# Decode kernel on one core: output weights loaded in wider rows with the attention output regrouped to match, half a head of them moved behind the last values, the last piece halved, the second K load in one piece, x loaded a second time

## The chip, the core and the metric

The kernel runs on one core of a Trainium2 chip. The metric is the device time of one execution in microseconds (us). A page called "the profile" is one execution taken by the hardware profiler; its span is about 2 us shorter than the time of the same execution. In this document PE is the matmul engine, DVE and ACT the two elementwise engines, SP the engine that issues nearly all loads.

## The reference, cut to what matters

One decode step: layer norm of one row x (448 wide), an attention over a cache of 65536 positions with 16 query heads in 8 K/V heads of width 256, an output projection, and a small gated feed-forward on the same row.

```python
xn = _layernorm(A_x)
q  = xn @ wq                                   # 448 -> 16 x 256
o  = softmax(q k^T / 16) v                     # k_cache, v_cache: 8 x 65536 x 256, bf16
y  = (silu(xn @ w_gate) * (xn @ w_up)) @ w_down * sigmoid(xn @ w_r)
out = x + o.reshape(1, 4096) @ wo + (xn + y)   # wo: 4096 x 448
```

K and V together are 537 MB of the 549 MB that are read. Every byte is used once.

## The kernel before

One ring of three 8 MB slots takes the loads: two slots for K, one for V (names in the code: `NT` = 28 value loads of the first seven heads, `U` = 4 loads of K for a head). SP issues all of them in order on one queue, each after a wait for the slot to come free. The first K loads come in two halves so that PE can start early:

```python
def k_item(u):
    need = [("FREE", u - 2)] if u >= 2 else ()
    if 2 <= u < UH:                                   # UH = 5: loads 0..4 are halved
        need = {0: [("FREEH", u - 2)], 1: need}
    slot_item("k", u, u % 2, [("slot%d" % (u % 2), CH), ("half%d" % (u % 2), CH)] if u < UH else None, need)
```

At the end the freed V slot takes the feed-forward weights and the output weights of seven heads, one load a head. The rows of one head are spread so that partition p holds rows p*2 and p*2+1 of each of the two query heads: two runs of 2 x 448 x 2 = 1792 bytes.

```python
def wo_src(h):
    return A_wo[h * rep * Dh:(h + 1) * rep * Dh, :].rearrange("(i p f) n -> p i f n", i=rep, f=NH)
...
slot_item("v", NT, 0, None, [("FREE", NU - 2)])
item("wg", ...gate and up weights...)
item("wd", ...two loads...)
item("wo", [(wo_view(wo_all[:, h * WON:(h + 1) * WON]), wo_src(h), "wo") for h in range(Hkv - 1)])
slot_item("v", NT + 1, ...); slot_item("v", NT + 2, ...)
slot_item("v", NT + 3, 2, ...six pieces of 64, 32, 16, 8, 4, 4 rows..., [("ATTN",), ("FFN2",)])
for i in range(rep):                                  # eighth head: two pieces, the very last loads
    item(("wo_end", i), [(wo_view(wo_end)[:, i, :, :], wo_src(Hkv - 1)[:, i, :, :], "we%d" % i)], ...)
```

Behind the last values come the last steps: normalise the attention output (tile oT_sb), multiply it with the eighth head's weights into ps_s ("the last matmuls"), copy the result, store it.

## Time and profile before

| | before |
|---|---|
| time, median (lowest to highest) | 1278.09 us of 3 runs (1277.79 to 1279.21); 1278.49 with the next three |
| span of the profile | 1276.0 us |
| DMA row, 40 slices | 9 in 39 of 40, then 8 |
| packets of 1792 bytes | 2048 of about 12,200 data packets |
| values' last landing / last weights' landing / result copy | 1272.23 / 1273.36 / 1273.98 us |

From the page: the DMA row of the 40 slices (tenths of the time that the 16 DMA engines were busy), the packet counts, and the chain of waits, followed back from the last instruction.

```profile
DMA  9999999999999999999999999999999999999998
...
DMA packets 13588, 549.20 MB, mean 430 GB/s; under 512 B 1414, under 2 KB 3464, under 8 KB 4104
...
DMA 76%; PE 19%; SPq 2%; ACT 1%; issue 1%; DVE 1%; ACTq 0%; DVEq 0%
```

The loads fill the span. The trace also records every packet (start, duration, size) and, for every load, the landing on each of the 16 engines. In the packet records the 16 engines hold a packet from about 1.8 us to 1272 us. One packet of 65536 bytes takes 2.422 us on the mean, and none of the 7424 in this trace took less than 2.418, so the 16 move 433 GB/s with such packets; over the whole span it was 430. There is next to nothing to win but packet cost, idle engines at the start, and the tail.

The timeline of SP as the feed-forward and output weights are issued (start, duration, engine, operation; merged rows):

```profile
1183.56 0.91 SPq L883 DMA_DIRECT2D ring<-in_B_w_down_dram  x2
1184.51 19.69 SPq L883 DMA_DIRECT2D ring<-in_A_wo_dram  x7
1204.24 0.99 SPq L883 DMA_DIRECT2D ring<-in_A_v_cache_dram  x1
```

It looks as if 19.69 us of issuing were a cost. But in the packet records at least 16 packets were under way at every moment of that time, mostly of loads issued earlier. So SP's standing there cost the loads nothing. The first two of the seven issues took 0.43 and 0.47 us, the third 7.16; that the queue had no room for more is my reading.

The timeline of PE, its weight loads (PEld) and DVE at the end (the square brackets tell the idle time before the row and what ended it; some rows left out):

```profile
1272.28 0.38 PE L412 MATMUL ps_m<-p_sb,ring 128*128 128x2 bf16 x8 [0.25 <-DMA ring<-in_A_v_cache_dram]
...
1272.80 0.16 DVE L654 TENSOR_TENSOR oT_sb<-ps_m,rs 128x4 bf16<-128x4 f32 x1 [0.48 <-PE ps_m L412]
...
1273.02 0.92 PE L412 MATMUL ps_s<-kt_all,oT_sb 128*1 128x224 bf16 x8 [0.25 <-DVE oT_sb L654]
1273.40 0.09 PEld L412 LDWEIGHTS ps_s<-kt_all,oT_sb 128*1 128x1 bf16 x4 [0.30 <-DMA kt_all<-in_A_wo_dram]
...
1273.98 0.38 DVE L835 CAST kt_all<-ps_s 33x224 bf16<-33x224 f32 x1 [1.02 <-PE ps_s L412]
```

The eight last matmuls start when the attention is ready (oT_sb); the second four of them start at 1273.40, when the last weights have landed (1273.36). Both arrive together, within about 0.1 us.

### The profile page before, as it was taken

The page shows a single profiled execution, that of the slowest core. Times are in us where ns is not written, and L with a number is a line of the kernel's source. Part 1 is how long each engine was busy: PE and PEld are TensorE (multiplying, and loading weights), DVE is VectorE, ACT ScalarE, POOL GpSimd, SP SyncE. Part 2 cuts the span into 40 slices and gives each one's busy share as a digit, 9 for nine tenths or more (in the row PEclk, how much of TensorE's full clock was granted, in tenths as well). Part 3 has the DMA queues.
Part 4 walks back from the last instruction along what each step waited for, and adds up shares of the span by engine and source line. Part 5 has one row for each costly group of instructions (what it writes and reads, how often), then busy time and mean ns, then how long its engine had stood idle before and what let it go on. Part 6 is the DMA issues. An engine that isn't in the chain of part 4 may idle for free.

```text
span 1276.0 us, 23620 instructions
## 1 busy us (share of the span) xinstructions
PE 976.1 (76%) x9791; PEld 638.2 (50%) x9791; DVE 570.2 (45%) x1079; ACT 436.6 (34%) x655; POOL 8.0 (1%) x38
## 2 busy tenths in 40 slices
PE   4998888778777679767778776787777688777674
PEld 3676655455544456444555454455454455454321
DVE  4665554355444455343454344454344554444310
ACT  1554533244333334323333342343333334332300
POOL 2000000000000000000000000000000000000000
PEclk9998999799888898887898888898888998888885
DMA  9999999999999999999999999999999999999998
GB/s 405 430 428 440 437 431 436 431 429 440 433 429 438 427 440 433 431 438 427 436 436 431 438 429 431 438 431 431 438 427 438 436 431 438 427 436 438 409 434 360
DMA packets 13588, 549.20 MB, mean 430 GB/s; under 512 B 1414, under 2 KB 3464, under 8 KB 4104
## 3 DMA queue, kind: packets, MB, share of 16 engines
q1 hardware_dynamic: 13570, 549.03, 99.7%
q8 instruction: 8, 0.13, 0.0%
q14 instruction: 4, 0.03, 0.0%
q10 hardware_dynamic: 6, 0.00, 0.0%
HBM read 549.03 MB, written 0.00 MB: 430 GB/s over the span
## 4 chain that ended last, share of the span: by engine, by line
DMA 76%; PE 19%; SPq 2%; ACT 1%; issue 1%; DVE 1%; ACTq 0%; DVEq 0%
DMA ring<-in_A_v_cache_dram 70%; PE ps_o L412 13%; DMA ring<-in_A_k_cache_dram 5%; PE ps_t L412 3%; SPq L883 2%; PE ps_m L412 2%; PE ps_q L412 2%; ACT kt_all L482 1%; DMA ring<-in_A_wo_dram 1%; DVE kt_all L480 0%; ACT S_sb L563 0%; PE ps_s L412 0%; DVE kt_all L699 0%; DVE m1p L533 0%; DVE kt_all L835 0%
## 5 line engine op out<-in xcount | busy, mean ns | idle before, releaser
L412 PE MATMUL ps_t<-ident_f,ring 128*128 128x128 f32 x4096 | 590.0, 286 | 71.9 <-DMA ring<-in_A_k_cache_dram 48.3
L480 DVE COPY kt_all<-ps_t 128x1024 bf16<-128x1024 bf16 x768 | 486.9, 684 | 285.8 <-PE ps_q L412 281.2
L412 PEld LDWEIGHTS ps_t<-ident_f,ring 128*128 128x128 f32 x4096 | 453.9, 144 | 227.6 <-issue 139.8
L482 ACT ACTIVATE kt_all<-ps_t 128x1024 bf16<-128x1024 bf16 x256 | 262.2, 1024 | 507.0 <-PE ps_q L412 506.9
L412 PE MATMUL ps_o<-ring,p_sb 128*4 128x512 bf16 x2044 | 186.9, 531 | 195.6 <-DMA ring<-in_A_v_cache_dram 191.3
L412 PEld LDWEIGHTS ps_o<-ring,p_sb 128*4 128x4 bf16 x2044 | 55.2, 105 | 289.5 <-issue 265.7
L412 PE MATMUL ps_q<-kt_all,q_cur 128*2 128x512 bf16 x2056 | 164.7, 397 | 0.6 <-DVE kt_all L480 0.6
L504 ACT ACTIVATE s<-ps_q 98x512 bf16<-98x512 f32 x257 | 151.8, 591 | 1.3 <-PE ps_q L412 1.3
L588 DVE RECIPROCAL rs<-ps_m 128x4 f32<-128x4 f32 x29 | 5.3, 183 | 271.8 <-PE ps_m L412 271.8
L573 ACT ACTIVATE p_sb<-S_sb 128x128 bf16<-128x128 bf16 x64 | 18.9, 307 | 266.2 <-PE ps_o L412 266.0
L412 PEld LDWEIGHTS ps_s<-sel_bf,s 128*128 128x128 bf16 x1032 | 64.2, 97 | 6.3 <-ACT s L504 1.9
L412 PE MATMUL ps_s<-sel_bf,s 128*128 128x8 bf16 x1032 | 63.4, 167 | 2.3 <-ACT s L504 1.3
L631 DVE CAST ob_sb<-ps_o 100x512 bf16<-100x512 f32 x29 | 20.1, 692 | 100.7 <-PE ps_o L412 100.7
L412 PEld LDWEIGHTS ps_q<-kt_all,q_cur 128*2 128x2 bf16 x2056 | 26.4, 79 | 45.5 <-issue 45.5
L412 PEld LDWEIGHTS ps_m<-rowsum,ones_f 128*128 128x128 f32 x116 | 20.1, 246 | 20.5 <-issue 20.5
L412 PE MATMUL ps_m<-rowsum,ones_f 128*128 128x2 f32 x116 | 22.5, 299 | 0.0
L533 DVE TENSOR_REDUCE m1p<-S_sb (+1 forms) x33 | 13.9, 422 | 4.4
L482 ACT ACT_TABLE_LOAD x7 | 9.0, 1283 | 19.1 <-PE ps_q L412 19.1
L531 DVE CAST S_sb<-ps_s 128x256 f32 (+1 forms) x33 | 13.6, 414 | 1.9 <-PE ps_s L412 1.9
L563 ACT ACTIVATE S_sb<-S_sb,negmax 128x512 bf16<-128x512 bf16 x16 | 13.2, 852 | 3.0 <-DVE negmax L557 3.0
L412 PE MATMUL ps_m<-diag,ones_f 2*128 2x2 f32 x58 | 11.0, 256 | 3.7 <-DVE diag L548 0.6
L412 PEld LDWEIGHTS ps_m<-diag,ones_f 2*128 2x128 f32 x58 | 8.5, 182 | 10.5 <-DVE diag L548 10.5
(94 smaller groups left out, 129.3 us busy)
## 6 DMA issues: line engine op xcount, KB each, us to landing
ring<-in_A_k_cache_dram SPq DMA_DIRECT2D x10, 4096.0 KB, 35.1
ring<-in_A_v_cache_dram SPq DMA_DIRECT2D x1, 4096.0 KB, 30.9
ring<-in_A_wq_dram SPq DMA_DIRECT2D x1, 3584.0 KB, 11.3
ring<-in_A_wo_dram SPq DMA_DIRECT2D x7, 448.0 KB, 17.1
ring<-in_A_v_cache_dram SPq DMA_DIRECT2D x1, 2048.0 KB, 35.5
ring<-in_B_w_gate_dram SPq DMA_DIRECT2D x1, 1568.0 KB, 14.9
ring<-in_B_w_up_dram SPq DMA_DIRECT2D x1, 1568.0 KB, 18.3
ring<-in_B_w_down_dram SPq DMA_DIRECT2D x2, 784.0 KB, 20.5
```

The costliest lines, as they stand in the source:

```text
L412: return pe.matmul(*a, **k)
L480: O(e, ("EV", s, m), lambda it: nc.vector.tensor_copy(out=kt[:, :], in_=tb[:, :]), f"ev{m}")
L482: O(e, ("EV", s, m), lambda it: nc.scalar.activation(out=kt[:, :], in_=tb[:, :], func=ACTF.Copy), f"ev{m}")
L504: O("act", ("EVQ", s), lambda it: nc.scalar.activation(out=s2[s % 2][0:QROWS, :], in_=ps_q[0:QROWS, :], func=ACTF.Copy), "evq")
L531: O("dve", ("SCOPY", u), lambda it: nc.vector.tensor_copy(out=S_sb[:, at(it, SBN), :], in_=ps_sn), "sc")
L533: O("dve", ("SMAX", u), lambda it: nc.vector.tensor_reduce(out=m1p[:, :, at(it, 1)], in_=S_sb[:, at(it, SBN), :].rearrange("p n i -> p i n ...
L563: O("act", ("EXP", h, i), lambda it, i=i: nc.scalar.activation(out=S_sb[:, :, i], in_=S_sb[:, :, i], func=ACTF.Exp, bias=negmax[:, i:i + 1 ...
L573: O("act", ("PC", t, c), lambda it: nc.scalar.activation(out=p_sb[:, c, :, :], in_=S_sb[:, n:n + CH, :], func=ACTF.Copy), "pc")
L588: O("dve", ("RS", t), lambda it: nc.vector.reciprocal(out=rs[:, :, :], in_=ps_m[0:P, C_TOT:C_TOT + NH * rep]))
L631: O("dve", ("OB", t), lambda it: nc.vector.tensor_copy(out=ob_sb[0:OROWS, :], in_=ps_o[0:OROWS, :]))
L883: eng.dma_start(fn[0], fn[1]).then_inc(sems[sem], 16)
```

## The change

Its intent: fewer and larger packets, the attention's last steps hidden behind loads, and two matmuls instead of four behind the very last load. Core of the diff, cuts marked:

```diff
+    HALVED = (0, 2, 3, 4)
...
-        if 2 <= u < UH:
+        if u >= 2 and u in HALVED:              # second K load whole; its half semaphore is preset
-        ... if u < UH else None, need)
+        ... if u in HALVED else None, need)
+    semtot = {"half1": 16}; items[("k", 1, 1)] = ("half1", 16)
...
+    def wo_rows(h0, h1):                        # partition p: four neighbouring rows, 3584 bytes
+        return A_wo[h0 * rep * Dh:h1 * rep * Dh, :].rearrange("(h p f) n -> p h f n", p=P, f=FO)
...
-    item("wd", ...two loads...)
-    item("wo", ...seven loads in runs of 1792 bytes...)
+    item("wd", [...one load..., (x_again, A_x[0], "wd")])
+    item("wo", [...six heads in one load..., ...first half of the seventh head...])
...
-    slot_item("v", NT + 3, 2, ..., [("ATTN",), ("FFN2",)])
+    slot_item("v", NT + 3, 2, ..., [("SUM",)])
+    item("wx", [...second half of the seventh head...], [("HT",)])
+    ENDS = [(0, 0, NH), (1, 0, 1), (1, 1, NH)]  # eighth head: three pieces instead of two
+    for k, (i, f0, f1) in enumerate(ENDS):
+        item(("wo_end", k), [...])
...
-        O("dve", "OTH", ...copy of oT_f...)
+        O("pe", "REGROUP", ...8 small matmuls with every second column of the identity...)
+        O("dve", "OTH", ...copy of the regrouped tile...)
...
+        O("dve", "XN_AGAIN", ...); O("dve", "YX", ...)   # x and its norm added here
-        base column: 4 matmuls at the start, 4 at the end, 3 vector steps (removed)
-        TOT: two matmuls for each value load's row sums
+        TOT: one
```

The base column held x and its norm for the final sum.

More of the change, by code (lines that the diff above doesn't have):

```diff
@@ L76, in bass_parallel_sum__gqa_block_cached__moe_arch_mod__decode_kernel @@
     WQN, WGN, WDN, WON = RP * HqDh // 2, RP * F, FH * D, rep * NH * D
+    FO = rep * NH
     WOA = (Hkv - 1) * WON
-    assert WOA + WGN + 2 * WDN <= SLOT
+    WEN = WOA + WGN + 2 * WDN
+    assert WEN + 2 * D <= SLOT
     DC = D // 4
@@ L95, in bass_parallel_sum__gqa_block_cached__moe_arch_mod__decode_kernel @@
     wd_area = slots[2][:, WOA + WGN:WOA + WGN + 2 * WDN]
+    x_again = slots[2][0:1, WEN:WEN + D]
+    xn_again = slots[2][0:1, WEN + D:WEN + 2 * D]
     wo_end = kt_all[:, 0:WON]
@@ L129, in bass_parallel_sum__gqa_block_cached__moe_arch_mod__decode_kernel @@
     oT_f = S_("oT_f", [P, NH, Hkv - 1, rep], FP32)
-    oT_h = S_("oT_h", [P, NH, Hkv - 1, rep], BF16)
-    base_c = S_("base_c", [P, 4], FP32)
+    oT_h = S_("oT_h", [P, FO, Hkv - 1], BF16)
     KB = 2 * FB
@@ L138, in bass_parallel_sum__gqa_block_cached__moe_arch_mod__decode_kernel @@
     res_bf = kt_all[:, 3 * KB + 2 * D:3 * KB + 2 * D + DQ]
-    assert WON <= 2 * KB and 3 * KB + 2 * D + DQ <= NKT * 8 * P
+    wo_x = kt_all[:, 2 * KB:2 * KB + WON // 2]
+    assert WON // 2 <= KB and WON <= 2 * KB and 3 * KB + 2 * D + DQ <= NKT * 8 * P
     hT_sb = S_("hT_sb", [P, FH, 2], BF16)
@@ L143, in bass_parallel_sum__gqa_block_cached__moe_arch_mod__decode_kernel @@
     x_f, xc_f, xn_f = T_(D, FP32), T_(D, FP32), T_(D, FP32)
-    xnb_f = xc_f
-    base_f = xn_f
     xn_bf = T_(D)
@@ L166, in bass_parallel_sum__gqa_block_cached__moe_arch_mod__decode_kernel @@
     C_HT = C_Q
-    C_BASE = C_Q
     assert C_Q + NH * Hq + 4 <= C_BIG and C_HT + FK <= C_BIG and C_BIG + P <= 512
@@ L177, in SEM @@
         return name
-    for n_ in ["pe", "act", "dve", "pool", "qk", "jt", "evq", "exp", "pc", "qc", "sc", "w0", "out", "wq", "wg", "wo", "wd", "we0", "we1", "half0", "half1"]:
+    for n_ in ["pe", "act", "dve", "pool", "qk", "jt", "evq", "exp", "pc", "qc", "sc", "w0", "out", "wq", "wg", "wo", "wd", "we0", "we1", "we2", "wx", "half0", "half1"]:
         SEM(n_)
@@ L234, in bass_parallel_sum__gqa_block_cached__moe_arch_mod__decode_kernel @@
     late = []
-    semtot = {}
+    semtot = {"half1": 16}
+    items[("k", 1, 1)] = ("half1", 16)
     fed = {}
@@ L262, in flat_src, with wo_src, wo_at @@
         return src.rearrange("a b -> (a b)").rearrange("(p n) -> p n", p=P)
-    def wo_src(h):
-        return A_wo[h * rep * Dh:(h + 1) * rep * Dh, :].rearrange("(i p f) n -> p i f n", i=rep, f=NH)
+    def wo_src():
+        return A_wo[(Hq - rep) * Dh:Hq * Dh, :].rearrange("(i p f) n -> p i f n", i=rep, f=NH)
     def wo_view(t):
         return t.rearrange("p (i f n) -> p i f n", i=rep, f=NH)
+    def wo_rows(h0, h1):
+        return A_wo[h0 * rep * Dh:h1 * rep * Dh, :].rearrange("(h p f) n -> p h f n", p=P, f=FO)
+    def wo_at(h, f):
+        return wo_all[:, (h * FO + f) * D:(h * FO + f + 1) * D]
     def k_item(u):
         need = [("FREE", u - 2)] if u >= 2 else ()
-        if 2 <= u < UH:
+        if u >= 2 and u in HALVED:
             need = {0: [("FREEH", u - 2)], 1: need}
-        slot_item("k", u, u % 2, [("slot%d" % (u % 2), CH), ("half%d" % (u % 2), CH)] if u < UH else None, need)
+        slot_item("k", u, u % 2, [("slot%d" % (u % 2), CH), ("half%d" % (u % 2), CH)] if u in HALVED else None, need)
     def v_item(t):
-        slot_item("v", t, 2, None, [("VFREE", t - 1)] if t else [("BASECOL",), ("QT",), ("R",), ("CONST",)])
+        slot_item("v", t, 2, None, [("VFREE", t - 1)] if t else [("QT",), ("R",), ("CONST",)])
     item("wq", [(wq_area, flat_src(A_wq, WQN), "wq")])
@@ L291, in bass_parallel_sum__gqa_block_cached__moe_arch_mod__decode_kernel @@
     item("wg", [(wg_area[:, 0:WGN // 2], flat_src(B_w_gate, F), "wg"), (wg_area[:, WGN // 2:WGN], flat_src(B_w_up, F), "wg")], [("VFREE", NT - 1)])
-    item("wd", [(wd_area[:, i * WDN:(i + 1) * WDN], B_w_down.rearrange("(s p t) n -> s p (t n)", s=2, p=P)[i], "wd") for i in range(2)])
-    item("wo", [(wo_view(wo_all[:, h * WON:(h + 1) * WON]), wo_src(h), "wo") for h in range(Hkv - 1)])
+    item("wd", [(wd_area.rearrange("p (s x) -> p s x", s=2), B_w_down.rearrange("(s p t) n -> p s (t n)", s=2, p=P), "wd"), (x_again, A_x[0], "wd")])
+    HL = Hkv - 2
+    item("wo", [(wo_all[:, 0:HL * WON].rearrange("p (h x) -> p h x", h=HL), wo_rows(0, HL).rearrange("p h f n -> p h (f n)"), "wo"),
+                (wo_all[:, HL * WON:HL * WON + WON // 2], wo_rows(HL, HL + 1)[:, 0, 0:FO // 2, :].rearrange("p f n -> p (f n)"), "wo")])
     slot_item("v", NT + 1, 1, None, [("FREE", NU - 1)])
     slot_item("v", NT + 2, 0, None, [("VFREE", NT)])
-    slot_item("v", NT + 3, 2, [("last%d" % k if k < len(LAST) - 1 else "slot2", J) for k, J in enumerate(LAST)], [("ATTN",), ("FFN2",)])
-    for i in range(rep):
-        item(("wo_end", i), [(wo_view(wo_end)[:, i, :, :], wo_src(Hkv - 1)[:, i, :, :], "we%d" % i)],
-             [("H", 0), ("H", 1)] if i == 0 else ())
+    slot_item("v", NT + 3, 2, [("last%d" % k if k < len(LAST) - 1 else "slot2", J) for k, J in enumerate(LAST)], [("SUM",)])
+    item("wx", [(wo_x, wo_rows(HL, HL + 1)[:, 0, FO // 2:FO, :].rearrange("p f n -> p (f n)"), "wx")], [("HT",)])
+    ENDS = [(0, 0, NH), (1, 0, 1), (1, 1, NH)]
+    for k, (i, f0, f1) in enumerate(ENDS):
+        item(("wo_end", k), [(wo_view(wo_end)[:, i, f0:f1, :], wo_src()[:, i, f0:f1, :], "we%d" % k)])
     for g, e in enumerate(("sp", "act")):
@@ L335, in pool_setup @@
         alias("pool", "CONST")
-        O("pool", "z_q", lambda it: v.memset(q_cur[:, :, :], 0.0))
+        O("pool", "z_q", lambda it: v.memset(q_cur[:, :, :], 0.0), "half1", 16)
         O("pool", "KZ", lambda it: v.memset(kt_all[:, :], 0.0))
@@ L376, in dve_setup @@
         alias("dve", "XE")
-        O("dve", "xnbf32", lambda it: v.tensor_copy(out=xnb_f, in_=xn_bf))
-        W("dve", "xnbf32")
-        O("dve", "BASE0", lambda it: v.tensor_tensor(out=base_f, in0=x_f, in1=xnb_f, op=ALU.add))
-        W("dve", "BASE0")
         O("dve", "R", lambda it: v.tensor_tensor_reduce(out=x_f, in0=xn_bf, in1=wr_row, scale=1.0, scalar=0.0,
@@ L400, in act_setup @@
         W("dve", "QT")
-        W("dve", "BASECOL")
         O("dve", "QTSB", lambda it: nc.vector.tensor_scalar(
             out=qT_sb[:, :, :], in0=ps_m[0:P, C_Q:C_Q + NH * Hq].rearrange("p (q f) -> p f q", f=NH), scalar1=inv_sqrt_dh, scalar2=None, op0=ALU.mult), "pc", 2)
-        O("dve", "BASEC", lambda it: nc.vector.tensor_copy(out=base_c[0:DC, :], in_=ps_m[0:DC, C_BASE + NH * Hq:C_BASE + NH * Hq + 4]))
         W("act", "QTSB")
@@ L444, in pe_setup @@
         O("pe", "QT", qt, "qk", 2)
-        W("pe", "BASE0")
-        W("pe", "R")
-        def basecol(it):
-            for c in range(4):
-                ins = mm(ps_m[0:DC, C_BASE + NH * Hq + c:C_BASE + NH * Hq + c + 1], lhsT=base_f[0:1, c * DC:(c + 1) * DC], rhs=ones_f[0:1, 0:1],
-                         start=True, stop=True)
-            return ins
-        O("pe", "BASECOL", basecol)
         W("pe", "PSQ_ZERO")
@@ L458, in pe_setup @@
         W("pe", "KZ")
+        W("pe", "z_q")
     def ev_engine(m):
@@ L579, in f @@
         def f(it):
-            for f_ in range(NH):
-                ins = mm(ps_m[0:P, C_TOT + f_ * rep:C_TOT + (f_ + 1) * rep], lhsT=ones_f[:, :], rhs=rowsum[:, :],
-                         start=True, stop=True)
-            return ins
+            return mm(ps_m[0:P, C_TOT:C_TOT + NH * rep].rearrange("p (f i) -> p f i", f=NH), lhsT=ones_f[:, :],
+                      rhs=rowsum[:, :].unsqueeze(1).to_broadcast([P, NH, rep]), start=True, stop=True)
         O("pe", ("TOT", t), f)
@@ L661, in pe_attn, with regroup @@
         W("dve", "OTF", NH - 1)
-        O("dve", "OTH", lambda it: nc.vector.tensor_copy(out=oT_h[:, :, :, :], in_=oT_f[:, :, :, :]))
+        W("pe", "OTF", NH - 1)
+        HN = Hkv - 1
+        def regroup(it):
+            for i in range(rep):
+                for r in range(rep):
+                    for hf in range(NH):
+                        c = C_BIG + (r * NH + hf) * HN
+                        ins = mm(ps_m[i * P // rep:(i + 1) * P // rep, c:c + HN], lhsT=ident_f[:, r:P:rep], rhs=oT_f[:, hf, :, i],
+                                 start=True, stop=True, tile_position=(0, i * P // rep))
+            return ins
+        O("pe", "REGROUP", regroup)
+        W("dve", "REGROUP")
+        O("dve", "OTH", lambda it: nc.vector.tensor_copy(
+            out=oT_h[:, :, :], in_=ps_m[:, C_BIG:C_BIG + FO * HN].rearrange("p (f h) -> p f h", f=FO)))
         W("pe", "OTH")
         W_item("pe", "wo")
-        todo = [(h, i, hf) for h in range(Hkv - 1) for i in range(rep) for hf in range(NH)]
-        O("pe", "ATTN", lambda it: [mm(ps_a, lhsT=oT_h[:, hf, h, i:i + 1], rhs=wo_view(wo_all[:, h * WON:(h + 1) * WON])[:, i, hf, :],
-                                       start=(h, i, hf) == todo[0], stop=(h, i, hf) == todo[-1]) for h, i, hf in todo][-1])
+        todo = [(h, f) for h in range(HN) for f in range(FO) if h < HN - 1 or f < FO // 2]
+        O("pe", "ATTN", lambda it: [mm(ps_a, lhsT=oT_h[:, f, h:h + 1], rhs=wo_at(h, f),
+                                       start=(h, f) == todo[0], stop=(h, f) == todo[-1]) for h, f in todo][-1])
     def pe_ffn1():
@@ L794, in ending @@
         pe_ffn2()
+        W_item("dve", "wd")
+        O("dve", "XN_AGAIN", lambda it: nc.vector.tensor_scalar(out=xn_again, in0=x_again, scalar1=stat[0:1, 7:8], scalar2=stat[0:1, 4:5],
+                                                                op0=ALU.add, op1=ALU.mult))
+        W("dve", "XN_AGAIN")
         W("dve", "FFN2")
@@ L797, in ending @@
         W("dve", "SIG")
-        O("dve", "YS", lambda it: nc.vector.tensor_scalar(out=sum_f, in0=ps_y, scalar1=stat[0:1, 6:7], scalar2=None, op0=ALU.mult))
+        O("dve", "YS", lambda it: nc.vector.scalar_tensor_tensor(
+            out=sum_f, in0=ps_y, scalar=stat[0:1, 6:7], in1=xn_again, op0=ALU.mult, op1=ALU.add))
         W("dve", "YS")
+        O("dve", "YX", lambda it: nc.vector.tensor_tensor(out=sum_f, in0=sum_f, in1=x_again, op=ALU.add))
+        W("dve", "YX")
         O("dve", "SUM", lambda it: nc.vector.tensor_tensor(out=sum_f, in0=ps_a, in1=sum_f, op=ALU.add))
@@ L806, in fin_base @@
             for g in range(NF):
-                for c in range(4 // NF):
-                    mm(fin(g)[:, c * DC:(c + 1) * DC], lhsT=base_c[0:DC, g * (4 // NF) + c:g * (4 // NF) + c + 1], rhs=ident_f[0:DC, 0:DC],
-                       start=(c == 0), stop=False, tile_position=(0, 32 * g), skip_group_check=True)
-                ins = mm(fin(g), lhsT=ones_f[0:1, 0:1], rhs=sum_f[:, g * DQ:(g + 1) * DQ], start=False, stop=False,
+                ins = mm(fin(g), lhsT=ones_f[0:1, 0:1], rhs=sum_f[:, g * DQ:(g + 1) * DQ], start=True, stop=False,
                          tile_position=(0, 32 * g), skip_group_check=True)
@@ L820, in ending, with fin_x, f @@
         pe_oT(T)
+        W_item("pe", "wx")
+        def fin_x(it):
+            for f in range(FO // 2):
+                for g in range(NF):
+                    ins = mm(fin(g), lhsT=oT_h[:, FO // 2 + f, HL:HL + 1], rhs=wo_x[:, f * D + g * DQ:f * D + (g + 1) * DQ], start=False, stop=False,
+                             tile_position=(0, 32 * g), skip_group_check=True)
+            return ins
+        O("pe", "FIN_X", fin_x)
         W("pe", "OTSB", T)
-        for i in range(rep):
-            W_item("pe", ("wo_end", i))
-            def f(it, i=i):
+        for k, (i, f0, f1) in enumerate(ENDS):
+            W_item("pe", ("wo_end", k))
+            def f(it, k=k, i=i, f0=f0, f1=f1):
                 wo = wo_view(wo_end)
-                for hf in range(NH):
+                for hf in range(f0, f1):
                     for g in range(NF):
                         ins = mm(fin(g), lhsT=oT_sb[:, hf, i:i + 1], rhs=wo[:, i, hf, g * DQ:(g + 1) * DQ], start=False,
-                                 stop=(i == rep - 1 and hf == NH - 1), tile_position=(0, 32 * g), skip_group_check=True)
+                                 stop=(k == len(ENDS) - 1), tile_position=(0, 32 * g), skip_group_check=True)
                 return ins
-            O("pe", ("FIN", i), f)
-        W("dve", "FIN", rep - 1)
+            O("pe", ("FIN", k), f)
+        W("dve", "FIN", len(ENDS) - 1)
         O("dve", "RESULT", lambda it: nc.vector.tensor_copy(out=res_bf[0:FROWS, :], in_=ps_s[0:FROWS, 0:DQ]))
```

## The prediction

> **What bounds the kernel: the loads.** In the page's 40 slices the DMA row is 9 in every slice but the last; the chain of waits is 76% DMA. The trace's DMA packet records are sharper: from 1.8 to about 1272 us of the span all 16 DMA engines hold a packet. A 65536-byte packet takes 2.422 us on one engine, 27.06 GB/s, times 16 is 433 GB/s[...]. Only bytes, cost per packet and the tail after the last landing can move the time. The stage that looks worst, 19.7 us of issuing seven output-weight loads (one took 7.16 us; "SPq" in the chain), is [...] worth nothing.
>
> **Cost per packet.** Means by size: 1792 B 78 ns, 6272 B 242, 12544 B 475; at 27.06 GB/s the bytes alone are 66, 232, 464, so each packet pays about 10 ns. One 448 KB part of the output weights lands 1.20 us after another: 16 packets per engine, 75 ns each.
>
> **The change in the loads, per engine.**
> - Six heads in rows of 3584 B: 8 packets of an estimated 141 ns instead of 16 of 75, 0.07 us per head: -0.43 us.
> - Second K load in one piece (8 packets of 2.422 us for 16 of 1.218): -0.11.
> - Last piece halved, rows of 896 B: 16 packets of about 42 ns for 8 of 75: +0.07.
> - x again: one packet, 40 ns: 0 to +0.04.
> - Half a head moved behind the last values: order only.
> Sum: about -0.45 us.
>
> **The tail.** Before: last values landed at 1272.23, attention (oT_sb) ready 1272.96, last weights landed 1273.36, last four matmuls 1273.40 to 1273.94, result copy 1273.98, end 1276.0. Weights and attention arrived nearly together. After: values land about 1.8 us before the last weights, attention is ready about 1 us early: the loads decide. Two matmuls instead of four follow the last landing; pairs start 0.14 us apart: -0.14 us.
>
> **Off the path.** Regrouping (8 small matmuls), normalising x again and one more vector add: about 2 us of DVE and PE work between 1208 and 1234. They delay the issue of the last values from 1231.3 to an estimated 1234; their turn comes near 1252. With K piece 1 whole, PE starts it about 2.7 us later (52 instead of 49.7), but PE waited 5.1 us for the fourth K load at 100.4, which absorbs it. The removed base-column matmuls (at 18 us) held up nothing: PE waited for K until 23.6.
>
> **Prediction.** 1278.1 - 0.45 - 0.14 = 1277.5 us, range 1276.5 to 1278.4. Faster by over 2% 0.005, within 2% 0.99, slower 0.005.
>
> **What would show each step.** All engines busy to the end; 1408 fewer packets under 2 KB and 768 more of 3584 B at 138 to 145 ns; last weights landing near 1272.9; result copy 0.43 us after the last matmuls start; the wait for the fourth K load down to about 2.4 us; last values issued near 1234 with no idle DMA.
>
> **What would make it wrong.** Start-up slack smaller than I read, so that the late K piece starves the queue (+1 to 3 us); the 768-packet load blocks the sync queue so long that the next values come late; one slow engine, not the mean, sets the end; 896-byte rows cost far more than 42 ns.

The 141 and 42 ns are estimates from the 75 ns of a 1792-byte packet, with 66 ns for 1792 bytes more and 33 for 896 bytes fewer.

## The result

| | before | after |
|---|---|---|
| time, median, same rounds (6 runs each) | 1278.49 us (1277.79 to 1279.67) | 1277.70 us (1277.34 to 1278.29) |
| span of the profile | 1276.0 | 1275.8 |
| packets of 1792 / 896 / 3584 bytes | 2048 / 2 / 0 | 384 / 259 / 768 |
| last weights landed, mean of the 16 engines / last engine | 1272.60 / 1273.36 | 1272.13 / 1273.20 |
| result copy | 1273.98 | 1273.70 |

The ratio of the times is 0.9993, with a 95% interval of 0.998 to 1.0006: the same at 2%, and not separated from no change at all. Ratios here are the mean time of one kernel's runs over that of the other's runs of the same rounds, so not quite the ratio of the medians that are quoted.

The page after, lines that answer to those shown before:

```profile
DMA  9999999999999999999999999999999999999998
...
DMA packets 12742, 549.20 MB, mean 430 GB/s; under 512 B 1335, under 2 KB 1978, under 8 KB 3386
...
DMA 80%; PE 17%; issue 1%; ACT 1%; DVE 1%; SPq 0%; ACTq 0%; DVEq 0%
```

846 packets fewer in all. "SPq" is gone from the chain, yet SP still stands 13.49 us at the output weights and no longer matters even in the picture:

```profile
1182.86 13.49 SPq L910 DMA_DIRECT2D ring<-in_A_wo_dram  x2
1196.40 9.46 SPq L910 DMA_DIRECT2D ring<-in_A_v_cache_dram  x2
```

The end, after:

```profile
1271.56 0.37 PE L420 MATMUL ps_m<-p_sb,ring 128*128 128x2 bf16 x8 [0.29 <-DMA ring<-in_A_v_cache_dram]
...
1272.07 0.16 DVE L651 TENSOR_TENSOR oT_sb<-ps_m,rs 128x4 bf16<-128x4 f32 x1 [0.52 <-PE ps_m L420]
...
1272.13 0.54 PE L420 MATMUL ps_s<-kt_all,oT_h 128*1 128x224 bf16 x4
...
1272.74 0.91 PE L420 MATMUL ps_s<-kt_all,oT_sb 128*1 128x224 bf16 x8
...
1273.24 0.08 PEld L420 LDWEIGHTS ps_s<-kt_all,oT_sb 128*1 128x1 bf16 x2 [0.21 <-DMA kt_all<-in_A_wo_dram]
...
1273.70 0.38 DVE L862 CAST kt_all<-ps_s 33x224 bf16<-33x224 f32 x1 [1.46 <-PE ps_s L420]
```

Attention is ready at 1272.23, a microsecond before the last weights (1273.20), and the tail hangs on loads alone. The same is told by the chain of waits of the last microseconds: before, it passes from the last values through the attention's matmuls and oT_sb,

```profile
1233.60 38.63 DMA ring<-in_A_v_cache_dram
1272.23 0.05 issue
1272.28 0.49 PE ps_m L412 x12
1272.78 0.02 issue
1272.80 0.17 DVE oT_sb L654
```

and after, it passes from weights straight into matmuls. The weights of this piece are the second half of the seventh head (landed at 1272.09); the three pieces of the eighth head landed behind them, at 1272.61, 1272.90 and 1273.20, and the last two matmuls waited for the last one (the row at 1273.24 above):

```profile
1237.23 34.86 DMA kt_all<-in_A_wo_dram
1272.09 0.04 issue
1272.13 0.54 PE ps_s L420 x4
```

### The profile page after: what moved, and what is told of

The parts are those of the page before. It is cut to its first block, busy times and chain, and to the rows that moved or that the text cites. A ratio compares the mean times of both kernels' runs of the same rounds, so it can differ in the third digit from the quotient of the medians.

```text
span 1275.8 us, 23503 instructions
## 1 busy us (share of the span) xinstructions
PE 956.0 (75%) x9735; PEld 624.7 (49%) x9735; DVE 570.3 (45%) x1078; ACT 436.2 (34%) x655; POOL 8.0 (1%) x38
## 4 chain that ended last, share of the span: by engine, by line
DMA 80%; PE 17%; issue 1%; ACT 1%; DVE 1%; SPq 0%; ACTq 0%; DVEq 0%
DMA ring<-in_A_v_cache_dram 68%; PE ps_o L420 12%; DMA ring<-in_A_k_cache_dram 7%; DMA kt_all<-in_A_wo_dram 3%; DMA ring<-in_A_wo_dram 2%; PE ps_t L420 2%; PE ps_q L420 1%; PE ps_m L420 1%; ACT kt_all L481 1%; SPq L910 0%; DVE kt_all L479 0%; ACT S_sb L562 0%; PE ps_s L420 0%; DVE kt_all L712 0%; DVE kt_all L815 0%
## 5 line engine op out<-in xcount | busy, mean ns | idle before, releaser
L420 PE MATMUL ps_o<-ring,p_sb 128*4 128x512 bf16 x2044 | 177.1, 508 | 204.6 <-DMA ring<-in_A_v_cache_dram 200.3
L420 PEld LDWEIGHTS ps_m<-rowsum,ones_f 128*128 128x128 f32 x58 | 12.3, 264 | 22.6 <-issue 22.6
L420 PE MATMUL ps_m<-rowsum,ones_f 128*128 128x4 f32 x58 | 14.8, 326 | 0.0
```

Source lines behind the costliest of these rows:

```text
L420: return pe.matmul(*a, **k)
```

## The experiments

Times scatter by more than the effects: the unedited kernel before, run as an experiment, came out at ratio 0.9996 of itself (interval 0.9981 to 1.0011). So the verdicts rest on the trace's landing records, split into three stages that are each far more repeatable than the time. All are differences of means over the 16 engines, except the lag. The times come from several sets of rounds on different chips, in which before's own median was 1278.49 (the result), 1279.19 (after_again, before_again, rows1792, rows512), 1279.50 (k3_whole, k1_halved, one_engine, wx_first), 1278.93 (end_whole, rows_only) and 1278.53 (k1_only, one_late); medians of different sets are compared with that in mind.

- Start: from the first to the second value load's landing (the only place, seen before the output weights, where kernels with the same loads differ by more than 0.1 us).
- Late: from the up-weights' landing (near 1200 us) to the last weights' landing.
- Lag: how far the slowest engine's last landing is behind the mean.

| kernel | time, median | start | late | lag | result copy |
|---|---|---|---|---|---|
| before (first profile) | 1278.49 | 77.66 | 72.04 | 0.76 | 1273.98 |
| before_again | 1278.43 | 77.81 | 72.05 | 0.85 | 1274.28 |
| after (first profile) | 1277.70 | 77.67 | 71.62 | 1.07 | 1273.70 |
| after_again | 1277.82 | 77.59 | 71.62 | 1.19 | 1273.81 |
| rows1792 | 1278.14 | 77.67 | 72.07 | 0.92 | 1274.04 |
| rows512 | 1281.45 | 77.78 | 74.46 | 2.59 | 1278.18 |
| rows_only | 1279.33 | 78.27 | 71.50 | 2.25 | 1275.71 |
| k1_halved | 1278.77 | 78.10 | 71.62 | 1.14 | 1274.38 |
| k1_only | 1277.89 | 77.69 | 72.01 | 0.92 | 1273.99 |
| k3_whole | 1286.84 | 85.48 | 71.64 | 1.58 | 1282.05 |
| wx_first | 1277.56 | 77.59 | 71.55 | 1.01 | 1273.54 |
| end_whole | 1277.68 | 77.60 | 71.60 | 1.01 | 1273.42 |
| one_engine | 1277.98 | 77.60 | 72.10 | 1.15 | 1274.20 |
| one_late | 1278.52 | 77.72 | 72.26 | 0.86 | 1274.11 |

The theory: the 16 engines always have packets to move (from about 1.8 to 1272 us in the trace of before), so packet cost and the tail are all that the change can move. Rivals: SP's issuing was the cost; moving half a head behind the values is the gain; the difference is chance.

### Repeats: after_again, before_again

No edit.

> The changed kernel, unedited. Theory (cost per packet, then the tail): 0.5 to 0.7 us faster than before in time; the mean over the 16 engines of the last weights' landing 0.45 us earlier than before's (1272.60). Rival (the pair of times differed only by chance): no difference outside 0.3 us in the timed runs, and the mean landing no earlier. A second trace also shows how much the slowest engine's lag behind the mean (0.76 us before, 1.07 us after) changes from run to run.

> The kernel before, unedited. Both theories: the same time within 0.5 us. It is there for a second trace: mean landing of the last weights 1272.60 within 0.1 us if that mean is a property of the kernel; its slowest engine may lag by another amount than 0.76 us if the lag is chance.

after_again: ratio 0.9989 (0.9975 to 1.0003), median 1277.82 against 1279.19 us for before in those rounds. The late stage is 71.62 in both traces of the changed kernel and 72.04 and 72.05 in both of before: 0.42 us, repeatable to 0.01. The mean last landing of before was 1272.80 instead of 1272.60, outside the 0.1 us that was expected; 0.15 of those 0.2 us arose in the start stage (77.81 for 77.66). So in the late stage there is a difference, it is no chance, and before has a second, variable loss that the first prediction did not know.

### The rows: rows1792, rows512, rows_only

rows1792 and rows512 are the changed kernel with the same bytes cut smaller:

```diff
-    item("wo", [(wo_all[:, 0:HL * WON].rearrange("p (h x) -> p h x", h=HL), wo_rows(0, HL)..., "wo"),
+    CUT = 896          # rows1792: 1792 bytes; rows512: CUT = 256
+    item("wo", [(wo_in[:, :, c:c + CUT], wo_from[:, :, c:c + CUT], "wo") for c in range(0, WON, CUT)] + [
```

> The changed kernel, its six heads of output weights loaded in rows of 1792 bytes again (two loads), all else kept. Theory: 8 more packets per head and engine, landing of the weights and everything after 0.4 us later on the mean engine, 1536 packets of 1792 B more and 768 of 3584 B fewer; time +0.4 us. Rival (the regrouping or the number of issues gives the gain, not the packets): landing unchanged.

> The changed kernel, six heads in pieces of 512 bytes (seven loads), the same bytes to the same places. Theory: 56 packets of about 29 ns per head and engine instead of 8 of 141: about +0.5 us per head, +2.9 us for six, in the mean landing and in the time. Rival (bytes alone count, the queue being full): +0.0. If the issuing queue is what limits (the rival that its 19.7 us mattered), engines would show idle time in this stage.

The 29 ns are an estimate: 512 bytes at 27.06 GB/s (19 ns) and the 10 ns that a packet paid in the trace of before.

rows1792: late stage 72.07, so +0.45 us, expected +0.4; that is before's 72.04 again. rows512: late stage 74.46, so +2.84 us, expected +2.9. The queue line of the page tells the packets apart:

```profile
DMA packets 17446, 549.20 MB, mean 429 GB/s; under 512 B 1431, under 2 KB 7450, under 8 KB 8090
```

The match is closer than the theory deserves. When the weights had landed, the mean engine was 2.38 us behind (13.96 us after the up-weights, for 11.58 in after); the other 0.48 us came with the value load behind them (19.47 us after the weights, for 18.93 to 19.15 in the other traces with the same order). SP spent even longer at the weights than before (24.48 us in the row below, five of the seven loads) and issued that value load only at 1211.12, 3.4 us ahead of the weights' mean landing, where before had 8.7 and after 15.7. The packet records show no idle engine from 1186 to 1206 us, but from there to 1220 an idle time of 0.16 us per engine, and two packets of 2.9 us instead of 2.42. So for before and after, with no idle engine in this stage, the rival of the issuing queue falls; here a still longer stand had begun to cost. Packet cost stands, at two sizes.

```profile
1182.82 24.48 SPq L913 DMA_DIRECT2D ring<-in_A_wo_dram  x5
```

Its time rose by 3.6 us (medians against after_again), 0.8 us more than the late stage: the slowest engine lagged by 2.59 us in the profile. That engine lost about 1.45 us in one stretch (11.15 us between two landings where the others took about 9.7). In that stretch, at 1260.42 us, the trace has an instruction fetch of 16384 bytes, 1.0 us long, with a data packet behind it 0.5 us longer than its kind. That the two are one is likely and not shown, since packets are not marked with their engine.

rows_only is before with nothing but the rows and the regrouping, for all seven heads:

```diff
-    item("wo", [(wo_view(wo_all[:, h * WON:(h + 1) * WON]), wo_src(h), "wo") for h in range(Hkv - 1)])
+    item("wo", [(wo_all[:, h * WON:(h + 1) * WON], A_wo[h * rep * Dh:(h + 1) * rep * Dh, :].rearrange("(p f) n -> p (f n)", p=P), "wo") for h in range(Hkv - 1)])
+        ... regroup, and oT_h[:, f, h:h + 1] in ATTN ...
```

> The kernel before with nothing but the rows of 3584 bytes and the regrouping for seven heads, still seven loads. Theory: mean last landing 0.4 to 0.5 us earlier than before, no change of the tail; time -0.4 to -0.5 us. Rival (the parts in the tail give the gain): within 0.1 us of before.

The late stage shrank by 0.54 us, a little more than expected (seven heads, all of it in wide rows), still with seven loads, so the number of issues is not what gives the gain. The time did not: ratio 1.0003, median 1279.33 us, and the mean last landing was 1272.83. Its start stage was the longest of all but k3_whole (78.27, 0.6 us longer than in the first trace of before), and its slowest engine lagged 2.25 us. So the term is right and a launch's other losses hid it; why this kernel's four timed runs (1278.57 to 1279.75) were all on the slow side stays open.

### The second K load: k1_halved, k3_whole, k1_only

k1_halved is the changed kernel with the second K load in halves again:

```diff
-    HALVED = (0, 2, 3, 4)
+    HALVED = (0, 1, 2, 3, 4)
-    semtot = {"half1": 16}; items[("k", 1, 1)] = ("half1", 16)
+    semtot = {}
```

> The changed kernel with the second K load in two halves again. Theory: mean landing of every later load 0.1 us later, PE waits about 5 us for the fourth K load instead of 1.1, time +0.1 us, which the timed runs cannot resolve. Rival (the whole second load costs start-up time): time falls by more than 0.3 us.

The landing of the last weights moved by 0.59 us (1272.72 for 1272.13), not 0.1, and all but 0.16 of it in the start stage (78.10 for 77.67). This refuted my reading of that stage as "absorbed". The timeline shows why. Granted PE clock and busy time around the fourth K load, before, after and in k1_halved (columns: window, length, busy of PE, PEld, DVE, ACT, POOL, clock as a share, then the DMA's; a packet counts in the window where it starts, so a short window's DMA share can pass 1):

```profile
100.00:102.00 2.00, 1.54 (x7) 1.55 (x8) 0.00 (x0) 0.00 (x0) 0.00 (x0) 0.50 0.84 360
102.00:104.00 2.00, 2.00 (x13) 0.82 (x13) 0.50 (x1) 0.51 (x1) 0.00 (x0) 0.50 1.03 442
```

```profile
100.00:102.00 2.00, 1.58 (x17) 0.97 (x17) 0.26 (x1) 0.00 (x0) 0.00 (x0) 1.00 0.95 410
102.00:104.00 2.00, 1.91 (x23) 1.81 (x20) 1.82 (x3) 1.60 (x3) 0.00 (x0) 1.00 0.95 410
```

```profile
100.00:102.00 2.00, 1.18 (x6) 1.18 (x7) 0.00 (x0) 0.00 (x0) 0.00 (x0) 0.50 0.95 410
102.00:104.00 2.00, 2.00 (x14) 0.82 (x13) 0.14 (x1) 0.15 (x1) 0.00 (x0) 0.50 1.07 459
```

With a halved second load PE has to wait 5 to 7 us for the fourth one and restarts at half clock, 20 matmuls in four microseconds instead of 40. The timeline's rows for that restart, before and after:

```profile
100.46 1.97 PE L412 MATMUL ps_t<-ident_f,ring 128*128 128x128 f32 x8 [5.09 <-DMA ring<-in_A_k_cache_dram]
```

```profile
100.42 1.09 PE L420 MATMUL ps_t<-ident_f,ring 128*128 128x128 f32 x8 [1.06 <-DMA ring<-in_A_k_cache_dram]
```

In the clock records the granted clock is 0.50 in stretches of 3.41 us or a multiple of it (3.41, 6.83 and 13.65 us in before, all but the one at the end of the record), which begin in each of the four waits of 5.1 to 6.7 us for the fourth K load and go on behind it: in before the wait is from 95.37 to 100.46 us and the half clock from 97.39 to 104.22. (Shorter waits went both ways, see the end.) With the second load whole, the long wait (4.0 us, to 51.91 in after) and the half clock (49.97 to 56.80) come before that load, where there is time to spare. PE then gets through the fourth load sooner, although it started the second one later, and SP issues the sixth K load sooner (it waits for the slot):

```profile
124.61 0.33 SPq L883 DMA_DIRECT2D ring<-in_A_k_cache_dram  x1
```

```profile
123.04 0.33 SPq L910 DMA_DIRECT2D ring<-in_A_k_cache_dram  x1
```

In the four traces with a halved second load this issue came at 124.61, 125.16, 125.88 and 125.35 us, and the start stage lost 0.07, 0.22, 0.68 and 0.51 us against the shortest one seen (77.59). In the seven traces of changed kernels that kept the clock at 1.00 there it came at 122.95 to 123.23 us, and the stage lost 0.00 to 0.19.

What counts is how early a load is issued, against the mean landing of the load ahead of it. Issued 5.2 to 5.6 us ahead, a load landed 19.33 to 19.35 us after that one (the sixth K load in these seven traces, and the second value load in four of them); 3.6 to 4.1 us ahead it took 19.35 to 19.54, 3.2 to 3.4 us ahead 19.46 to 19.75, and 2.8 us ahead 19.69 and 19.72 (k3_whole, below, is left out). Three of the seven (after, rows1792, rows512) lost their 0.08 to 0.19 at the second value load: the clock was at 0.50 near 139 us too, and SP issued it at 144.2 to 144.3 instead of 142.4 to 142.7. That the half clock makes the issue of the sixth K load late fits the times (from PE's start on the fourth load to this issue 24.2 to 25.0 us in the four traces, 22.6 in the seven), but no run changes the clock alone.

With a late issue the queue is nearly dry (3.3 us ahead in k1_halved, under two packets of 2.42 us for each engine). There, packets of 65536 bytes took up to 3.8 us near 128 us and up to 4.5 us near 147 us, where the sixth K load and the second value load begin, instead of 2.42. Hardly an engine looks idle; single packets last longer.

k3_whole amplifies the same margin: the fourth load is whole too.

```diff
-    HALVED = (0, 2, 3, 4)
+    HALVED = (0, 2, 4)          # half semaphore preset to 32
```

> The changed kernel with the fourth K load whole as well (the fifth and the first stay halved). Theory (the start-up has slack for the second K load only): PE starts the fourth K load at 110 instead of 100.4 us, frees its slot near 132.7 instead of 123, the engines run dry near 129 for about 4.7 us, and once more near 153 for 1 to 2 us; time +5 to +7 us. Rival (whole loads only save packets): -0.1 us and no idle engines.

Time 1286.84 us, 9.0 us above after_again and 9.3 above wx_first, which ran in the same rounds; the mean landing came 7.8 us later. Expected were 5 to 7. The windows view of k3_whole (DMA share is the last column but one):

```profile
125.00:128.00 3.00, 2.91 (x32) 2.19 (x31) 2.05 (x4) 1.68 (x3) 0.00 (x0) 1.00 0.81 350
128.00:131.00 3.00, 2.91 (x32) 2.19 (x31) 2.05 (x5) 1.68 (x3) 0.00 (x0) 1.00 0.00 0
131.00:134.00 3.00, 2.91 (x34) 2.18 (x32) 2.04 (x4) 1.67 (x3) 0.00 (x0) 1.00 0.00 0
134.00:137.00 3.00, 2.82 (x33) 2.06 (x30) 1.72 (x4) 1.63 (x3) 0.00 (x0) 1.00 0.97 350
```

No packet started for six microseconds: the sixth K load was issued at 134.08 instead of the 132.7 I had worked out. The 1.4 us fit the half clock again, after a wait of 11.3 us for the fourth load, which my sum left out (24.1 us from PE's start on that load to the issue, as in before, for 22.6 in after). So one late issue in the start-up can cost more than all the packets of the change gain.

k1_only is before with only the whole second load, to separate it from the removed base column, without which PE started on K up to 0.8 us earlier (22.75 for 23.59):

```diff
+    HALVED = (0, 2, 3, 4)       # and the half semaphore preset, as in the change; nothing else
```

> The kernel before with nothing but the second K load whole (base column, rows, tail as before). Theory formed from the runs so far (start-up margin): PE then waits about 4 us for the second K load, restarts at half clock there, and waits only about 1 us for the fourth, with the clock staying at 1.00; so it is done with the fourth K load near 123.2 us instead of 124.6 to 125.9, the sixth K load and second value load are issued in time, and the mean landings from first to second value load stay 77.6 us apart (77.7 to 78.3 in the kernels with a halved second K load). Time 0.2 to 0.8 us below before, and less spread. Rival (the base column's removal did it): still 124.6 or later and 77.7 or more; time within 0.1 us of before (packets alone).

A half success. Ratio 0.9997 (0.9984 to 1.0011), median 1277.89 against 1278.53 us: not resolved. The sixth K load came at 124.28 us, later than the 123.2 expected, because PE, not slowed at the second load (3.2 us of waiting, no half clock), came earlier to the fourth, waited 3.0 us and then was slowed (clock 0.50 for 3.41 us from 101.6). The start stage was 77.69. So the whole load alone removes the long wait, not the half clock; the base column's share of it is not excluded. In one run of the full change too, one_late, a wait of 1.73 us was followed by half clock, and the sixth load came at 124.52. The margin is better with the whole load, and not certain.

### The order and the last piece: wx_first, end_whole

wx_first loads all of the seventh head before the last values:

```diff
-    item("wo", [...six heads..., ...first half of the seventh...])
+    item("wo", [(wo_all.rearrange("p (h x) -> p h x", h=HL + 1), wo_rows(0, HL + 1)..., "wo")])
-    item("wx", ...); O("pe", "FIN_X", ...)
```

> The changed kernel with the whole seventh head loaded before the last values again (no part of it behind them). Theory: the order in the queue changes, not its end: last values land 0.57 us later than in the changed kernel, attention is ready near 1272.8 instead of 1272.2, the last weights land at the same time, and the first of the last matmuls starts up to 0.15 us later; time within 0.15 us. Rival (moving it hides the attention's last steps): +0.5 us.

Late stage 71.55, 0.07 us shorter than after (the seventh head now also travels in 3584-byte rows), result copy 1273.54, time 1277.56: nothing was lost by not moving it. Attention was ready at 1272.53, still 0.4 us before the last weights (1272.95). The rival of the moved half head falls.

end_whole leaves the last piece in one load:

```diff
-    ENDS = [(0, 0, NH), (1, 0, 1), (1, 1, NH)]
+    ENDS = [(0, 0, NH), (1, 0, NH)]
```

> The changed kernel with the last piece whole again (one load of 1792-byte rows, four matmuls behind it). Theory: the last weights land 0.07 us earlier, the result copy starts 0.58 us after the last load's matmuls begin instead of 0.44; net +0.07 us. Rival (halving gives most of the gain): +0.3 us or more.

Late stage 71.60 (0.02 us shorter, expected 0.07). The result copy came 0.45 us after the last landing (1273.42 to 1272.97), no later than in after (0.50), where it should have been 0.14 later. The reason is in the windows view of the last two microseconds, end_whole first, then after:

```profile
1272.00:1274.00 2.00, 0.97 (x12) 0.21 (x8) 0.39 (x2) 0.00 (x0) 0.00 (x0) 0.81 0.03 12
```

```profile
1272.00:1274.00 2.00, 1.48 (x14) 0.37 (x12) 0.46 (x2) 0.00 (x0) 0.00 (x0) 0.50 0.06 21
```

In that run PE's clock was up at the end (0.81), and matmul pairs started 0.09 us apart instead of 0.14. So halving the last piece is worth some 0.1 us at half clock, on paper, and whether the clock is up is worth as much. Its time, 1277.68, is that of after.

### One engine: one_engine, one_late

The prediction named "one slow engine, not the mean, sets the end" as a danger. Both kernels put 61 rows of 896 bytes on one engine. That they went to one is read from the packet records: 24 of these packets in a microsecond, one after another, 42 ns each.

```diff
+    (slots[2][0:61, WEN + 2 * D:WEN + 3 * D], A_wo[0:61, :], "wd")                   # one_engine: beside x
+    item("one", [(kt_all[1:62, 3 * KB:3 * KB + D], A_wo[0:61, :], "one")], [("HT",)]) # one_late: before the last values
```

> The changed kernel with one more load of 61 rows of 896 bytes beside the second load of x, which should fall on one engine [...]: about 2.5 us of packets there. Theory (the slowest engine sets the end): mean last landing +0.16 us, that engine's landing +2.5 us, the last landing +0.5 to +2.5 us according to where that engine stood (average engine: +1.4), time likewise. Rival (engines share the work, the mean decides): +0.16 us everywhere. It also shows that one extra packet of x can cost at most 0.04 us.

> The changed kernel with the 61 rows of 896 bytes for one engine (2.5 us there) put behind the third value load from the end, among 65536-byte packets. In the earlier run they stood before the output weights' small packets, and all engines came 0.48 us later, none 2.5. Theory A (the engines run apart when the packets are large): that engine's landings of the last values come 2.5 us later, the other fifteen unchanged within 0.1 us, last landing +0.5 to +2.0 us, time likewise. Theory B (engines are held together by the queue): all sixteen 0.16 to 0.5 us later, the last no more than that.

one_engine: late stage 72.10, +0.48 us; the last landing 1273.69, 0.38 to 0.49 later than in the two traces of after; lag unchanged. Neither number expected. one_late: the value load ahead of the rows landed 0.18 us later on the mean, the one behind them 0.57, and the last landing came 0.25 to 0.36 us later. The loaded engine had been among the earliest: its rows landed at 1252.07, so it had been free for them 2.56 us before, at about 1249.5, where the mean was 1250.7 and the last engine 1252.2. At the next load the last engine landed at 1261.93, which is where this engine had to be by addition. So one late engine is hidden by the lag of the others, which is theory A; but the others came later too (the median engine by 0.46 us at that load, 0.24 of it before the rows), which theory A does not have. Where the others lost it is in the packet records: while the 61 packets ran (1248.8 to 1251.4), the 21 packets of 32768 bytes that started beside them lasted 1.33 to 1.50 us instead of 1.21 (0.30 us per engine in all), and 65536-byte packets under way at that time cost about 0.14 more; with the 0.16 of the rows themselves that is 0.60 of the 0.64 us by which the late stage grew. In one_engine it was the 3584-byte packets: 150.7 ns on the mean for 144.4 in after, 48 to an engine, 0.30 us, and 0.46 of the 0.48 with the rows. Why packets last longer beside an engine that moves small rows stays open. One extra row of x, 0.04 us of one engine, is far below either.

No version was faster than the changed kernel beyond the scatter. wx_first and end_whole have shorter late stages and earlier result copies (by 0.16 and 0.28 us against the first trace of after) and the same times; at 1277.56 and 1277.68 us against 1277.70 and 1277.82 the difference is not resolved.

## Why the prediction was right

It said 1277.5 us (1276.5 to 1278.4), and 1277.70 was measured.

- Loads decide, packets are the term: right. Of the predicted -0.43 for rows, +0.07 for the halved piece and up to +0.04 for x, together -0.34 us in the late stage, -0.42 was measured in both pairs of traces; undone alone, the rows gave 0.45 back.
- SP's 19.7 us are worth nothing: right, no engine was idle beside them; but the margin is finite (rows512, 24 us and more: about 0.5 us lost at the next value load).
- Half a head behind the values changes order only: right, it even costs 0.07 us (wx_first).
- Tail -0.14 us: the copy came 0.50 us after the last landing instead of 0.62, so -0.12. The clock of PE can be worth the same (end_whole).
- "Last weights landing near 1272.9": wrong, it was 1273.20. The mean engine did what the sum said (1272.60 to 1272.13); the slowest one lagged 1.07 us instead of 0.76. The step that failed is the one from "per engine" to the landing of the last; it was named as a danger and its size was not given.
- "PE starts it about 2.7 us later, but PE waited 5.1 us for the fourth K load, which absorbs it": the direction was right (the wait shrank, to 1.06 us, not 2.4), the worth was wrong. The long wait was not harmless slack: the clock was 0.50 from within it to 3.8 us behind it in before, and the later issue that followed went with 0.07 to 0.68 us lost in the start stage in the traces with halves. The term was -0.11 us for packets (-0.07 measured in every trace, from the first weights to the first values); against k1_halved the whole load was worth 0.43 us more at the start, in one pair of traces, while in before alone (k1_only) it did not stop the half clock. The profile of before that I predicted from had, by luck, the smallest loss of the four traces with halves.
- "The removed base-column matmuls held up nothing": doubtful. PE started on K at 22.73 to 23.18 us in nine traces without them, at 23.49 in a tenth, and at 23.49 to 23.73 in the four with them; no run removes them alone.
- Last values issued near 1234 with no idle DMA (1234.24), 3584-byte packets of 138 to 145 ns (mean 144): as said. Those of 896 bytes took 41 ns, for about 42.
- Taken together, an estimate from the traces: 0.42 (late) + 0.07 (packets of K) + 0.12 (tail) + 0 to 0.7 (start) - 0.2 to 0.4 (lag), so 0.2 to 1.1 us. The medians differ by 0.79 and 1.37 us in the two sets of rounds. The total was right partly because the missing gain at the start and the larger lag pulled in opposite directions.

## What to carry to other kernels

When the DMA engines are full from end to end, cost a change in packets per engine and in the tail, and let waits that end before the queue runs dry count for nothing (here a load issued 5.2 us or more ahead of the landing before it lost nothing). But do not call a long wait of PE free slack: look at its clock behind it (0.50 behind the waits of 5.1 to 6.7 us here), and at the lead of the loads that it has to release next. And measure such small effects in landings averaged over the engines, stage by stage, since times of whole runs scattered by more than twice the effect.

## What else was measured here

- Cost of a packet: packets from 1792 to 12544 bytes paid 10 to 12 ns each: 78 ns for 1792 bytes, 142 (median, after) for 3584, 242 for 6272, 475 for 12544 (before), against 27.06 GB/s for the bytes alone.
- How far the 16 engines drift apart: landings of one load spread over about 1.7 us for a thousand microseconds (1.61 to 1.76 us from 150 to 1180 us in before and after), and the slowest engine was 0.76 to 2.6 us behind the mean at the end.
- What one engine's extra packets do to the others: 2.5 us put on one engine made the mean landing 0.48 and 0.64 us later in the two runs, not 0.16, and the last one 0.3 to 0.5 us; packets of 32768 bytes on the other engines lasted up to 1.50 us instead of 1.21 meanwhile (one_late).
- A load that is issued late: with the next load issued 3.3 us before the mean landing of the one ahead (k1_halved), single packets of 65536 bytes took up to 4.5 us instead of 2.42, with hardly an engine idle in the records; with 5.2 us and more nothing was lost.
- The clock of PE after a wait for the fourth K load: waits of 5 to 11 us were followed by half clock, and so were waits of 3.0 (k1_only) and 1.73 us (one_late), while waits of 0.59 to 1.71 us in seven other traces were not. How long a wait it takes is not settled by these.
- Instruction fetches in the DMA queues: eight packets of 16384 bytes in a run, about 1.0 us each.
